# The second product of a fused attention and feed-forward kernel, made product by product, its last ones in two levels of Strassen

## The chip, the cores and the metric

The kernel runs on one core of a Trainium2 chip. The metric is the device time of one execution in microseconds, taken as the median of several runs. All arithmetic is in 32-bit floats.

## The reference, cut to what matters

For 8 batches and 12 heads, sequence 448, head size 64: q and k are normalised by their root mean square and scaled by gains, softmax attention is taken over them, and its output, 3584 tokens by 768, goes through two products with a squared ReLU between them.

```python
q_n, k_n = rmsnorm(q, g_q), rmsnorm(k, g_k)
attn = softmax(q_n @ k_n.T / sqrt(64))
x = (attn @ v) as [3584, 768]
h = x @ w_in                 # 768 -> 2048
g = maximum(h, 0) ** 2
out = g @ w_out              # 2048 -> 768
```

## The kernel before, in words

**Spans.** The work goes in four spans of two batches. Both products are made by Strassen's scheme (Winograd's form): rows of w, depth and tokens are halved, and seven products of half size, named A11, A12, S2, S1, S3, A22 and S4 after the combination of weights that each uses, replace eight. The combinations of weights are prepared in the attention of span 0 and in its first product and lie in DRAM as w1s and w2s; those of x lie in xT and xC, those of g in gT and gC.

**First product** (`first_product`, matmuls at L1068). For each of eight blocks of 128 hidden units, seven products of three matmuls (128x128 weights, 448 tokens). VectorE and ScalarE empty PSUM, ScalarE applies the ReLU (L1040), GpSimd squares (L1044), VectorE makes the combinations of g (`combine`, L1028 to L1032). In spans 1 and 2 the first pairs of the next span's attention are normalised beside it (`ahead`).

**Second product** (`second_product`, matmuls at L1106). For each of three columns m of 128 output features in each half, seven products of eight matmuls, each eight into one PSUM bank; two banks alternate (`bank`). The order is a list, `uses2`: A11 and A12 for each m, then for each m S2, S1, S3, A22, S4. VectorE adds what comes out to p1, y or ct (L1117 to L1127); a finished block is turned by 32x32 transposes and stored by four DMAs (`deliver`, L1139 and L1142). In span 0 `combine` also runs here, beside the first eight of the products.

**What sets the order.** Everything is recorded in the order in which the Python code issues it, and each engine runs its instructions in that order. `second_product` and `attention` are generators: the main loop at the end takes one step of `attention` (61 steps and some at its end) and then as many matmuls of `second_product` as bring it in proportion to `total`. So the attention of the next span is spread over the second product of this one.

**One pair of heads** in `attention(first)`, i its number: scores of two chunks (L785) with their exponentials on ScalarE (L787), the values of pair i-1 (L862), scores of the other two, the copy of `rest` (L992); then, with product matmuls after each yield: `norm_by_squares(i + 2)`, `transposes(i + 1)`, sums of the probabilities and `finish(i - 1)` (L808 to L810, L898, L900), `squares(i + 3)` (ScalarE, L737), `fold(i)`, `combine_x(i - 1)`, and the two DMA steps from GpSimd's queue: factors to DRAM (L1016) and back, spread over partitions (`spread`, L830). `norm_by_squares` reduces on VectorE (L744), swaps neighbouring groups of 32 partitions by four 32x28 copies (L747), adds, scales (L748, L749), and lets GpSimd take the root and multiply (L750, L752). `fold` reduces the sums over partitions (L817), brings three groups of 32 partitions together by three 32x28 copies (L820), adds, inverts and turns them (L822 to L824). Loads of q, k, v, weights (`load_blocks`, L665, five blocks ahead) and the stores are issued by SyncE in order.

**Last product** (`last_product`, span 3, no attention beside it). It is already in two levels: for columns 0 and 1 each of the seven products is made by seven inner ones of four matmuls on 224 tokens (L1206), column 2 as before (L1234). Its inner sums of g are made by VectorE (`add_g`, L1192), those of weights by GpSimd (`add_weights`, L1180).

Of the kernel before, what the change touches and what calls it, by code (L numbers as in the profile page):

```python
# [10 lines left out]
F32 = mybir.dt.float32  # L11
U32 = mybir.dt.uint32
AF = mybir.ActivationFunctionType
ALU = mybir.AluOpType
# [373 lines left out]
def attention_then_ffn_bounded(  # L388
# [35 lines left out]
    nc = tc.nc  # L424
# [4 lines left out]
    P = 128  # L429
# [209 lines left out]
    written = [0]  # L639
    stream = []  # L640

    uses2 = [(m, i) for m in range(HC) for i in (A11, A12)]
    uses2 += [(m, i) for m in range(HC) for i in (S2, S1, S3, A22, S4)]
    def order_of(span, f):

        return (A11, A12, S2, S1, S3, A22, S4) if span == f == 0 else range(7)

    N1 = HF * 7
    N2 = HC * 7 * (HF // 4)

    def load_blocks(upto):

        while len(stream) < min(upto, NSPAN * (N1 + N2) - N2):
            n = len(stream) % (N1 + N2)
            if written[0] < min(2 * (n // 7 + 1) if n < N1 else 2 * NFC, 2 * NFC):
                return
            sw = loads.tile([P, 4, P], F32, tag="sw", name="sw", bufs=5)
            if n < N1:
                sw = sw[:, 0:HC]
                src = w1s[n // 7, order_of(len(stream) // (N1 + N2), n // 7)[n % 7]].rearrange("p (c m) -> p c m", c=HC)  # L660
            else:
                n -= N1
                m, i = uses2[n // (HF // 4)]
                src = w2s[i, n % (HF // 4), :, :, m * P:(m + 1) * P]
            nc.sync.dma_start(sw, src)  # L665
            stream.append(sw)

# [37 lines left out]
    def norm(i):  # L705
        if i >= NAT:
            squares(i)
            return norm_by_squares(i)
        raw, sq = (places_of(qk, i, n)[:SP] for n in range(2))
        rstd = rstds[i] = small.tile([SP, 2, 2 * NJ], F32, tag="rstd", name="rstd", bufs=4)  # L710
        normed[i] = sq[:, 0], raw[:, 1]
        if i <= 2:
            return normalise_in_turn(nc, raw, sq, rstd, mhalf)
        nc.scalar.activation(sq, raw, AF.Square)
        nc.vector.tensor_reduce(rstd, sq.rearrange("p s (n d) -> p s n d", d=D), AX, ALU.add)  # L715
        nc.vector.tensor_scalar(rstd, rstd, 1.0 / D, 1e-6, ALU.mult, ALU.add)
# [22 lines left out]
    def norm_by_squares(i):  # L739
        raw, qkn = (by_squares(i, n) for n in range(2))  # L740
        NG = S // 32
        half = small.tile([P, 2 * NG], F32, tag="half", name="half")
        other = small.tile([P, 2 * NG], F32, tag="other", name="other")
        nc.vector.tensor_reduce(half, qkn.rearrange("p s g e -> p (s g) e"), AX, ALU.add)  # L744
        for n in range(4):
            m = n ^ 1
            nc.vector.tensor_copy(other[n * 32:(n + 1) * 32], half[m * 32:(m + 1) * 32])  # L747
        nc.vector.tensor_tensor(half, half, other, ALU.add)  # L748
        nc.vector.tensor_scalar(half, half, 1.0 / D, 1e-6, ALU.mult, ALU.add)  # L749
        nc.gpsimd.tensor_tensor(half, half, mhalf, ALU.pow)  # L750
        for s in range(2):
            nc.gpsimd.tensor_tensor(  # L752
                qkn[:, s], raw[:, s],
                half[:, s * NG:(s + 1) * NG].rearrange("p g -> p g ()").to_broadcast([P, NG, 32]), ALU.mult)
        normed[i] = qkn
# [56 lines left out]
    def fold(i):  # L812


        NG = S // 32
        acc, quarters = sums["acc"].rearrange("p h q -> p (h q)"), sums["quarters"]
        nc.vector.tensor_reduce(quarters[:, 0], acc.rearrange("p (n k) -> p n k", k=32), AX, ALU.add,  # L817
                                apply_transpose=True)
        for n in range(1, 4):
            nc.vector.tensor_copy(quarters[0:32, n], quarters[n * 32:(n + 1) * 32, 0])  # L820
        square, turned = sums["square"][:, 0], sums["square"][:, 1]
        nc.vector.tensor_reduce(square[:, 0:2 * NG], quarters[0:32].rearrange("p a n -> p n a"), AX, ALU.add)  # L822
        nc.vector.reciprocal(square[:, 0:2 * NG], square[:, 0:2 * NG])
        nc.vector.transpose(turned, square)  # L824
# [147 lines left out]
    def attention(first):  # L972


        last = first + 2 * NPAIR
        for i in range(first, last + 1):
            if i < last:
                scores(i, 0)
                scores(i, 1)
            if i + 3 < min(last + 2, B * NPAIR):  # L980
                load(i + 3)
            if i == first:
                yield
            if i > first:
                values(i - 1)
            if i < last:
                add_up(i, 1)
                scores(i, 3)
                scores(i, 2)
            if i > first:  # L990
                rest = halves[(i - 1) % 2].rearrange("p h q -> p (h q)")
                nc.scalar.copy(rest, rests[i - 1])  # L992
                rests[i - 1] = rest
            if i + 2 < last:
                norm_by_squares(i + 2)
            yield
            if i + 1 < last:
                transposes(i + 1)
            if i < min(last, B * NPAIR - 1):
                load_v(i + 1)  # L1000
            yield
            if i < last:
                add_up(i, 2)
                add_up(i, 3)
            if i > first:
                finish(i - 1)
            if i + 3 < last:
                squares(i + 3)
            yield
            if i < last:  # L1010
                fold(i)
            if i > first:
                combine_x(i - 1)
            yield
            if i < last:
                nc.gpsimd.dma_start(sums["out"][i % 2], sums["square"][0:2 * S // 32, 1])  # L1016
                spread(i)
            yield
# [15 lines left out]
    def first_product(work, span):  # L1034
# [9 lines left out]
                nc.gpsimd.tensor_tensor(g, g, g, ALU.mult)  # L1044

        for f in range(HF):
            n = span * (N1 + N2) + f * 7
            order = order_of(span, f)
            g11, g12 = gT[:, f, 0:S], gT[:, f, S:2 * S]
            g21, g22 = gT[:, HF + f, 0:S], gT[:, HF + f, S:2 * S]  # L1050
# [39 lines left out]

    def second_product(work, span):

        B11, B21, B22 = gT[:, 0:HF, 0:S], gT[:, HF:, 0:S], gT[:, HF:, S:2 * S]
        T1, T2, T4, T3 = gC[:, 0], gC[:, 1], gC[:, 2], gT[:, 0:HF, S:2 * S]
        rhs_of = {A11: B11, S2: T2, S1: T1, S3: T3, A12: B21, A22: T4, S4: B22}
        n = span * (N1 + N2) + N1
        add = nc.vector.tensor_tensor
        done = []
        turn[0] += 1

        p1s = {}
        for j, (m, i) in enumerate(uses2):
            ps = bank("ps")
            for c in range(HF):
                load_blocks(n + 5)
                nc.tensor.matmul(ps, stream[n][:, c % 4], rhs_of[i][:, c], start=c == 0, stop=c == HF - 1)  # L1106
                n += c % 4 == 3
                if c == HF // 2 - 1 and done:
                    yield
                    deliver(work, span, *done.pop())  # L1110
                if span == 0 and j < 8 and c % 4 == 1:
                    combine(j % 4 * HF // 4 + c // 4, (j // 4,))
                if c < HF - 1:
                    yield
            if i == A11:
                p1s[m] = work.tile([P, S], F32, tag="p1", name="p1", bufs=HC)
                nc.scalar.copy(p1s[m], ps)  # L1117
            elif i == S2:
                add(p1s[m], p1s[m], ps, ALU.add)
            elif i == S1:  # L1120
                y = work.tile([P, S], F32, tag="y", name="y", bufs=1)
                add(y, p1s[m], ps, ALU.add)
            else:
                ct = work.tile([P, S], F32, tag="ct", name="ct", bufs=1)
                add(ct, p1s[m] if i in (A12, A22) else y, ps, ALU.add)
                if i == S3:
                    add(p1s[m], p1s[m], ps, ALU.add)  # L1127
                done.append((ct, m + (HC if i in (S3, A22) else 0), 1 if i in (S3, S4) else 0))
            yield
        if done:  # L1130
            deliver(work, span, *done.pop())
            yield


    rows = out.rearrange("(b g t) n -> b t g n", b=B, t=32)

    def deliver(work, span, ct, col, t, queues=(nc.sync,), part=slice(0, S // 32), kept=2):
        osb = work.tile([P, S // 32, 32], F32, tag="osb", name="osb", bufs=kept)[:, part]
        nc.vector.transpose(osb.rearrange("p g n -> p (g n)"), ct[:, part.start * 32:part.stop * 32])  # L1139
        for i in range(0, P, 32):  # L1140
            queue = queues[i // 32 % len(queues)]
# [224 lines left out]
    for span in range(NSPAN - 1):  # L1366
# [5 lines left out]
        with tc.tile_pool(name="second_product", bufs=2, reuse_waits="tile") as work:  # L1372
# [2 lines left out]
            places.append(qkT[:, 1])  # L1375
            halves[:] = [work.tile([P, 2, S // 2], F32, tag=f"half{m}", name="half", bufs=1) for m in range(2)]
            sums_for(work)
            total, done, most = HC * (7 * HF + 4) - 20, 0, 10 * NPAIR + 1
            for u, _ in enumerate(attention(nxt)):
                while done < total * min(u + 1, most) // most + 3 * max(u + 1 - most, 0):  # L1380
                    next(rest)
# [108 lines left out]
```

## Time and profile before

| what | value |
| --- | --- |
| time, median of 3 runs | 1353.98 us (1352.47 to 1356.12) |
| profiled execution | 1352.32 us, span 1350.1 us |
| PE busy | 1329.7 us of the span |
| second product and attention, spans 0, 1, 2 | 196.8, 196.9, 197.0 us |
| matmul 128x128x448, as two records | 0.376 us each in the chain |
| small copies of 32x28, L747 and L820 | 144 of 174 ns and 108 of 339 ns |
| exponential 128x896, L787 | 915 ns |
| root on GpSimd, L750 | 4869 ns |

A matmul of 32-bit floats shows as two records on PE. The profile's matmul durations overlap each other (543 ns on average where the next one starts 376 ns later), so the times between starts are what counts. PE is TensorE, PEld its weight loads, DVE is VectorE, ACT ScalarE, POOL GpSimd, SP SyncE. An instruction's idle time before it names what released it.

### The profile page before, as it was taken

The numbers are of one execution on the slowest core, as the hardware profiler recorded it, in microseconds if no ns is written. First come the engines' busy times: TensorE is split into PE (matmuls) and PEld (weight loads), VectorE is DVE, ScalarE is ACT, GpSimd is POOL, SyncE is SP. The second block draws the span as 40 slices with busy tenths as digits, with TensorE's granted clock in tenths as the row PEclk, the third lists the DMA queues.
The fourth block names the chain that finished last, engine by engine and source line by source line (L and its number), as shares of the span: only waits on it lengthen the run. The fifth ranks groups of instructions, "written<-read, shape, count | busy, mean of one in ns | idle before, by whom it ended". The sixth has DMA issues, their size and how long they took to land.

```text
span 1350.1 us, 17275 instructions
## 1 busy us (share of the span) xinstructions
PE 1329.7 (98%) x5786; PEld 671.6 (50%) x5786; DVE 873.4 (65%) x1537; ACT 431.8 (32%) x681; POOL 619.4 (46%) x504
## 2 busy tenths in 40 slices
PE   8999999999999999999999999999999999999997
PEld 3333445444444455444444455544444445556887
DVE  6999788599987333568777623457878743336553
ACT  7886466433332011233333111223333201111000
POOL 5767533466564122646556212446656412422452
PEclk9999999999999999999999999999999999999999
DMA  9877999655686333345676432345665444431333
GB/s 241 225 217 200 314 360 333 181 131 107 135 151 129 101 87 88 101 114 114 143 146 123 114 97 87 90 112 125 130 123 126 105 102 135 134 88 53 114 101 58
DMA packets 413814, 190.15 MB, mean 141 GB/s; under 512 B 282388, under 2 KB 408724, under 8 KB 413716
## 3 DMA queue, kind: packets, MB, share of 16 engines
q1 hardware_dynamic: 406164, 180.21, 52.0%
q0 software_dynamic: 4736, 8.40, 2.4%
q8 instruction: 48, 0.79, 0.3%
q10 hardware_dynamic: 2816, 0.34, 0.2%
q14 instruction: 50, 0.41, 0.1%
HBM read 155.72 MB, written 33.16 MB: 140 GB/s over the span
## 4 chain that ended last, share of the span: by engine, by line
PE 89%; DVE 5%; ACT 2%; DMA 1%; issue 1%; POOL 0%; SPq 0%; POOLq 0%; DVEq 0%
PE ps L1106 29%; PE pd L1068 10%; PE pa L1068 10%; PE pc L1068 10%; PE sc L785 7%; PE pav L862 7%; PE pb L1068 5%; PE ps L1234 3%; PE pd L1206 2%; PE pc L1206 2%; PE pa L1206 2%; DVE gT L810 1%; PE pb L1206 1%; DVE rstd L715 1%; ACT gT L797 1%
## 5 line engine op out<-in xcount | busy, mean ns | idle before, releaser
L1106 PE MATMUL ps<-gT,sw 128*128 128x448 f32 x576 | 225.8, 543 | 0.0
L1044 POOL TENSOR_TENSOR gT<-gT 128x448 f32<-128x448 f32 x96 | 94.1, 982 | 284.8 <-ACT gT L1040 284.8
L750 POOL TENSOR_TENSOR half<-half,mhalf 128x28 f32<-128x28 f32 x36 | 175.3, 4869 | 74.6 <-DVE half L749 74.0
L1106 PE MATMUL ps<-gC,sw 128*128 128x448 f32 x432 | 170.1, 543 | 0.0
L1106 PEld LDWEIGHTS ps<-gT,sw 128*128 128x128 f32 x576 | 107.5, 190 | 113.9 <-issue 110.1
L1068 PE MATMUL pa<-xT,sw 128*128 128x448 f32 x384 | 155.0, 540 | 0.6 <-ACT p L1072 0.6
L1040 ACT ACTIVATE gT<-gT 128x448 f32<-128x448 f32 x96 | 55.3, 576 | 313.4 <-DVE gT L1083 313.4
L1106 PEld LDWEIGHTS ps<-gC,sw 128*128 128x128 f32 x432 | 80.6, 190 | 86.3 <-issue 83.2
L787 ACT ACTIVATE pr<-sc 128x896 f32<-128x896 f32 x87 | 77.5, 915 | 124.1 <-PE sc L785 124.1
L785 PE MATMUL sc<-qkT 64*64 64x448 f32 (+1 forms) x1152 | 109.8, 496 | 0.0
L1068 PEld LDWEIGHTS pa<-xT,sw 128*128 128x128 f32 x384 | 72.8, 190 | 72.7 <-issue 70.1
L583 POOL TENSOR_TENSOR gC<-gC 128x384 f32<-128x384 f32 x64 | 76.2, 1208 | 62.2 <-DVE gC L579 60.4
L1083 DVE TENSOR_TENSOR gT<-z,pd 128x448 f32<-128x448 f32 x32 | 19.8, 619 | 97.8 <-PE pd L1068 97.7
L1068 PE MATMUL pd<-xT,sw 128*128 128x448 f32 x192 | 77.9, 542 | 1.3 <-DVE z L1075 1.3
L1068 PE MATMUL pd<-xC,sw 128*128 128x448 f32 x192 | 77.5, 540 | 1.3 <-DVE gT L1083 1.3
L830 POOL DMA_DIRECT2D xT<-factors x72 | 38.0, 532 | 88.4 <-DMA factors<-square 56.8
L1068 PE MATMUL pb<-xC,sw 128*128 128x448 f32 x192 | 77.5, 540 | 0.1
L1068 PE MATMUL pc<-xC,sw 128*128 128x448 f32 x192 | 77.4, 539 | 0.0
L1068 PE MATMUL pc<-xT,sw 128*128 128x448 f32 x192 | 77.4, 539 | 0.0
L752 POOL TENSOR_TENSOR qk<-qk,half 128x448 f32<-128x448 f32 x72 | 75.9, 1074 | 2.8
L862 PE MATMUL rest<-pr,vt 64*64 64x448 f32 x348 | 72.7, 537 | 0.0
L862 PE MATMUL pav<-pr,vt 64*64 64x448 f32 x348 | 72.7, 537 | 0.0
(233 smaller groups left out, 2159.2 us busy)
## 6 DMA issues: line engine op xcount, KB each, us to landing
sw<-w1s SPq DMA_DIRECT2D x224, 192.0 KB, 2.4
sw<-w2s SPq DMA_DIRECT2D x126, 256.0 KB, 3.3
w1s<-gC SPq DMA_DIRECT2D x8, 1344.0 KB, 7.1
w2s<-gC SPq DMA_DIRECT2D x8, 1344.0 KB, 6.3
out_dram<-osb SPq DMA_DIRECT2D x184, 56.0 KB, 1.8
qk<-in_q_dram SPq DMA_DIRECT2D x144, 56.0 KB, 3.4
qk<-in_k_dram SPq DMA_DIRECT2D x144, 56.0 KB, 2.8
xT<-factors POOLq DMA_DIRECT2D x72, 112.0 KB, 3.4
```

The lines of the kernel that those rows point to most:

```text
L583: nc.gpsimd.tensor_tensor(*[blocks_of(n)[:, place_of(n, i)] for i in (dst, x, y)], op)
L750: nc.gpsimd.tensor_tensor(half, half, mhalf, ALU.pow)
L752: nc.gpsimd.tensor_tensor(qkn[:, s], raw[:, s], half[:, s * NG:(s + 1) * NG].rearrange("p g -> p g ()").to_broadcast([P, NG, 32]), ALU.mult)
L785: nc.tensor.matmul(sc[part, h, 0:n], qkT[rows, 0, 1, keys], qkT[rows, 0, 0, of], start=True, stop=True)
L787: nc.scalar.activation(pr, sc[:, :, 0:n], AF.Exp)
L862: nc.tensor.matmul(into, vs[i][rows, h, c, :], probs[i, c][rows, h, :], start=(c == 0), stop=(c == NF), skip_group_check=True)
L1040: nc.scalar.activation(g, src, AF.Relu)
L1044: nc.gpsimd.tensor_tensor(g, g, g, ALU.mult)
L1068: nc.tensor.matmul(ps, stream[n + at][:, c], rhs[:, c], start=first and c == 0, stop=c == HC - 1, skip_group_check=not first)
L1106: nc.tensor.matmul(ps, stream[n][:, c % 4], rhs_of[i][:, c], start=c == 0, stop=c == HF - 1)
L1206: nc.tensor.matmul(ps, lhs[:, c], rhs[:, c], start=first and c == 0, stop=c == HK - 1, skip_group_check=not first)
L1234: nc.tensor.matmul(ps, weights_of(o, m, c // HK)[:, c % HK], rhs_of[i][:, c, part], start=c == 0, stop=c == HF - 1)
```

## The change

The second product goes product by product: for each of A11, A12, S2, S1, S3, A22, S4 the three columns m. The first `FIRST[span]` products (6, 5, 5) are made as before; the remaining ones, one in span 0 and two in spans 1 and 2, in two levels for columns 0 and 1 and plainly for column 2. Their weights for columns 0 and 1 are loaded whole into parts of gC that are free by then (`load_set`), inner combinations go to free rows of gT. The steps of the attention are shared over the first products alone (`total`). The four copies of `norm_by_squares` and the three of `fold` go from VectorE to ScalarE. What followed them is cut off into `scale_by_squares`, which comes after `transposes(i + 1)`, and `factors_of`, which comes after `combine_x` and just ahead of the factors' DMA.

```diff
+    FIRST = (6,5,5)
+    order2 = (A11, A12, S2, S1, S3, A22, S4)
...
+            plan += [(w2s[i, k, :, :, m * P:(m + 1) * P], 2 * NFC) for o, i in enumerate(order2)
+                     for m in range(HC) if o < FIRST[span] or m == HC - 1 for k in range(HF // 4)]
...
     def norm(i):
         if i >= NAT:
             squares(i)
-            return norm_by_squares(i)
+            norm_by_squares(i)
+            return scale_by_squares(i)
...
         for n in range(4):
             m = n ^ 1
-            nc.vector.tensor_copy(other[n * 32:(n + 1) * 32], half[m * 32:(m + 1) * 32])
+            nc.scalar.copy(other[n * 32:(n + 1) * 32], half[m * 32:(m + 1) * 32])
+        spare["halves", i] = half, other
+
+    def scale_by_squares(i):
...
         for n in range(1, 4):
-            nc.vector.tensor_copy(quarters[0:32, n], quarters[n * 32:(n + 1) * 32, 0])
+            nc.scalar.copy(quarters[0:32, n], quarters[n * 32:(n + 1) * 32, 0])
+
+    def factors_of(i):
...
             if i + 1 < last:
                 transposes(i + 1)
+            if i + 2 < last:
+                scale_by_squares(i + 2)
...
             if i < last:
+                factors_of(i)
                 nc.gpsimd.dma_start(sums["out"][i % 2], sums["square"][0:2 * S // 32, 1])
...
+        def load_set(o):
+            if o < end:
+                for k, (m, h) in enumerate(((0, 0), (0, 1), (1, 0), (1, 1))):
+                    nc.sync.dma_start(tiles[o][k], w2s[order2[o], h, :, :, m * P:(m + 1) * P])
+
+        def add_g(o, k):
...
+                dst, x, y = ((t1, b12, b11), (t2, b22, t1), (t3, b22, b12), (t4, b21, t2))[k]
+                nc.vector.tensor_tensor(dst, x, y, sub)
+
+        def add_weights(o):
...
+                nc.gpsimd.tensor_tensor(s1, a21, a22, add)
+                nc.gpsimd.tensor_tensor(a21, a11, a21, sub)
...
+        for o, i in enumerate(order2):
...
+            if o < first:
+                for m in range(HC):
+                    ps = bank("ps")
+                    for c in range(HF):
+                        load_blocks(n + 5)
+                        nc.tensor.matmul(ps, stream[n][:, c % 4], rhs_of[i][:, c], start=c == 0, stop=c == HF - 1)
+                        n += c % 4 == 3
+                        at = (o * HC + m) * HF + c
+                        if span == 0 and at < 8 * HF and at % 4 == 1:
+                            combine(at // 4 % HF, (at // 4 // HF,))
...
+                        if o == first - 1 and c == 5:
+                            if m < 2:
+                                load_set(first + m)
+                            for k in ((0, 1), (2,), (3,))[m]:
+                                add_g(first, k)
+                            if m == 2:
+                                add_weights(first)
...
+            pa = ps_s.tile([P, 2, 512], F32, tag="s", name="pa")[:, 0, left]
+            yield from run(pa, a11, lambda c: b11[:, c])
+            nc.scalar.copy(z, pa)
+            nc.gpsimd.tensor_tensor(a11, s1, a11, sub)
+            nc.gpsimd.tensor_tensor(s4, a12, a11, sub)
+            for k in range(3):
+                add_g(o + 1, k)
+            send(o)
...
+            third = work.tile([P, S], F32, tag="ct", name="ct", bufs=1)
+            nc.vector.tensor_tensor(third, base[2], ps, add)
+            pb = ps_o.tile([P, S], F32, tag="o", name="pb")[:, left]
+            yield from run(pb, a11, lambda c: t2[c])
+            nc.vector.tensor_tensor(z, z, pb, add)
...
+            pc = bank("pc")[:, left]
+            yield from run(pc, s1, lambda c: t1[c])
...
+            add_weights(o + 1)
...
+            pd = ps_o.tile([P, S], F32, tag="t", name="pd")[:, left]
+            yield from run(pd, a21, lambda c: t3[c])
...
+            yield from run(pa, a12, lambda c: b21[:, c], False)
...
+            yield from run(pd, a22, lambda c: t4[c], False)
...
+            yield from run(pc, s4, lambda c: b22[:, c], False)
...
-            total, done, most = HC * (7 * HF + 4) - 20, 0, 10 * NPAIR + 1
+            total, done, most = FIRST[span] * HC * HF - (20 if FIRST[span] == 7 else 6), 0, 10 * NPAIR + 1
```

## The prediction

> **What bounds the kernel now.** I read first the page's busy times, then its chain of work, then one stage after another.
>
> ```profile
> PE 1329.7 (98%) x5786; PEld 671.6 (50%) x5786; DVE 873.4 (65%) x1537; ACT 431.8 (32%) x681; POOL 619.4 (46%) x504
> PE 89%; DVE 5%; ACT 2%; DMA 1%; issue 1%; POOL 0%; SPq 0%; POOLq 0%; DVEq 0%
> ```
>
> TensorE is busy 98% of the span and the chain that ends last runs 89% on it, so a product that needs fewer columns is time saved, if TensorE is still fed. The busy times by stretch give the second-product stages of spans 0 and 1, then 15 us of span 0:
>
> ```profile
> 261.00:457.80 196.80, 196.80 (x1112) 91.83 (x1111) 164.46 (x317) 62.82 (x88) 104.13 (x79) 1.00 0.62 126
> 582.00:778.90 196.90, 196.90 (x1112) 91.96 (x1111) 148.01 (x290) 60.98 (x85) 101.18 (x78) 1.00 0.59 126
> 306.00:321.00 15.00, 15.00 (x91) 7.00 (x90) 14.51 (x29) 4.72 (x7) 8.70 (x6) 1.00 0.51 80
> ```
>
> After the stretch and its length come PE, PEld, DVE, ACT and POOL. PE has no gap in either stage, although VectorE is nearly full in the first pairs of span 0. What the new form costs is already in the trace: the last product of the kernel is made in it. The timeline of PE:
>
> ```profile
> 1226.13 1.68 PE L1206 MATMUL pa<-gT,qk 128*128 128x224 f32 x8
> 1227.64 6.18 PE L1234 MATMUL ps<-gT,qk 128*128 128x448 f32 x16
> 1233.66 1.68 PE L1206 MATMUL pb<-xC,qk 128*128 128x224 f32 x8
> ...
> 1242.74 1.68 PE L1206 MATMUL pa<-gT,wb 128*128 128x224 f32 x8
> ```
>
> From pa to the next pa is 16.61 us. Eight records of 224 columns take 1.51 us, sixteen of 448 take 6.02 (a matmul is two records: 0.376 us each at 448, 0.189 at 224). Half the columns cost half, and the weight loads of 0.190 us don't slow it.
>
> Then one pair of the attention inside the second product of span 1:
>
> ```profile
> 643.64 1.73 PE L785 MATMUL sc<-qkT 64*64 64x448 f32 x16
> 644.68 0.92 ACT L787 ACTIVATE qkT<-sc 128x896 f32<-128x896 f32 x1 [1.19 <-PE sc L785]
> 647.82 1.31 PE L785 MATMUL sc<-qkT 64*64 64x224 f32 x16
> 650.07 0.53 ACT L992 COPY half<-rest 128x448 f32<-128x448 f32 x1
> 656.54 1.10 DVE L817 TRANSPOSE_TENSOR_REDUCE quarters<-acc 128x28 f32<-128x896 f32 x1
> 657.67 0.57 DVE L820 COPY quarters<-quarters 32x28 f32<-32x28 f32 x3
> 659.03 1.73 PE L785 MATMUL sc<-qkT 64*64 64x448 f32 x16
> ```
>
> A pair starts with its scores at 643.64, the next at 659.03. The fold of the sums (L817) ends 1.4 us before that: VectorE runs a whole pair behind.
>
> [...] the 112x16 activation of L725 took 216 ns. [...] three copies of L820 took 0.57 us alone and 1.48 at 640.87 beside GpSimd's multiply L752 (mean 339 ns each). [...] Here the small factors DMA lands in 2.7, the spread in 3.4.
>
> **The change, part by part.**
>
> 1. Five products in two levels: S4 in span 0, A22 and S4 in spans 1 and 2. A plain product is 24 matmuls: 24 x 0.7515 = 18.04 us. A two-level one takes 16.61 to 16.73 in the last product (periods between its 448-wide blocks); I take 16.67. Saved 1.37 each, **6.8 us** in all, on the bound engine.
>
> 2. Their extra sums. Per product VectorE gets four 128x896 subtractions (L1192, 1.1 to 1.5 us) and some 4 us of smaller ones, about 10 us in 16.7; GpSimd four 128x512 sums (1.27 each) and three of 0.66. In the last product the same load cost TensorE 0.1 us here and there, which is in 16.67. Taken as 0, bounds 0 to 0.5 each: the cover is the 6.0 us block of the third column, made before pb needs the new weights. The new weight DMAs (4 x 256 KB) are issued one product ahead, and stream loads fall by the same number of blocks.
>
> 3. Order. Product by product instead of column by column changes neither matmuls nor evictions: 0. Deliveries bunch in the second product (A12) and S3, so SyncE holds 2.1 us of out DMAs per delivery ahead of the next q and k loads, and these feed the squares on ScalarE. In before such loads came up to 6.6 us into a pair and the squares 14.3 us into it, without harm to PE. Taken as 0, bounds 0 to 2.
>
> 4. The attention is packed tighter, since it ends before the two-level products. In before the first scores of two pairs are 14.64 or 15.40 us apart, with 12 or 13 product matmuls between them, so the pair itself takes 14.64 - 12 x 0.7515 = 5.62. Now 114 matmuls are shared over 61 steps, 5 to a pair: 9.34 x 0.7515 + 5.62 = **12.64 us** in spans 1 and 2; 138 in span 0 give 11.31 and 14.1 us. That is no gain or loss on TensorE; the question is whether the others follow. VectorE had 148.0 us in span 1. Less 12 x 1.7 of small copies, less 12.7 of evictions and deliveries that move behind the attention, plus 5 for the first subtractions of g: about 120 in 160 (120 matmuls, 90 us, and 12.5 pairs, 70), 75% as before. GpSimd: 4.83 + 2.1 + 0.6 + 1.05 and some 2.7 of waiting for the factors, 11.3 of 12.64.
>
> 5. Small copies. ScalarE gets 7 per pair, 1.5 us; it has 5.1 of 15 us busy. But they wait for VectorE in ScalarE's queue. Behind the three of the fold stand the exponentials of the next pair, for which TensorE waits. The chain from a pair's first score at 0: ScalarE ends the copy of rest at 6.96 (650.60), its four copies at 7.8; VectorE's root sums, 0.37, end at 8.2; two adds 1.08 + 1.27, finish 1.25, fold 1.10 and gaps, 4.9: 13.1; three copies and two handoffs of 0.05: **13.85**. The next exponential would start at 12.64 + 1.04 = 13.68, so it is 0.2 late, and 0.8 to 1.4 late where an eviction (0.6) and a delivery (0.64) lie in the chain. TensorE notices when a score buffer isn't free: the third scores start 4.18 into the pair (647.82), so the exponential may start at 3.2 instead of 1.04, 2.1 late. The margin is 0.7 to 1.9 us. Other chain: square ends 14.8, GpSimd is free of its multiply at about 15.3, factors and spread take 3.1 + 3.7, landed at 22.1, 9.5 into the next pair; wanted at 11.3. I take 0.7 us of stalls in spans 1 and 2 together, bounds 0 to 12. In span 0 VectorE also combines g over the first 64 matmuls; before, its fold slipped to 3.0 us into the next pair with no stall. The same slip now delays the exponential to about 5.0, where 3.2 is allowed; but the pair's work falls by 1.7 us of copies to about 14.3 in 14.1, so I let it slip by half: 0.6 us, bounds 0 to 5.
>
> 6. The first product. Four times (two in spans 1 and 2 each) a norm sits before z. In before:
>
> ```profile
> 541.57 0.78 DVE L747 COPY other<-half 32x28 f32<-32x28 f32 x4
> 542.69 0.61 DVE L1075 TENSOR_TENSOR z<-p,pb 128x448 f32<-128x448 f32 x1
> 543.36 2.52 PE L1068 MATMUL pd<-xT,sw 128*128 128x448 f32 x6
> ```
>
> pd came 0.18 late (a block takes 2.44 instead of 2.25 in the chain), because z empties its bank. The copies become 4 x 0.21 plus two handoffs of 0.05, 0.94 in place of 0.78: 0.2 us more each time, **0.8 us** lost. Bounds 0 and, at 0.3 per copy, 2.
>
> Sum: -6.8 + 0.7 + 0.6 + 0.8 = **-4.7 us**. The profiled run took 1352.32 us, span 1350.1 plus 2.2; its span becomes 1345.4. The median of the runs shown is 1.66 above that run: 1353.98 - 4.7 = **1349.3 us**.
>
> **Rivals.**
>
> A. Nearly all of the gain arrives: no stall at all, 1347.2. For it: PE idles nowhere in the stages of before, even behind a full VectorE. I count it with the forecast.
>
> B. Half or more is eaten by waits in the tight pairs: late factor DMAs (landings of the spread up to 5.6 us, against margins of 1.8, and 0.7 where GpSimd has a difference of x to make) and the slip in span 0. 3 to 6 us go: 1350 to 1353, about 1352. Against it: these delays fall in few pairs.
>
> C. Slower: the exponentials queued behind the fold's copies become a ring with VectorE. It decides once the chain of 13.85 grows by more than the 0.7 to 1.9 us of margin, in every pair: from there each us is a us per pair. Copies of 0.35 instead of 0.21 add 1.0[...]. Then 0.5 us in 32 pairs, 16 us, less 6.8 - 0.8: 1354 + 10 = 1364. Against it: the chain is caught again in each pair, as the root sums wait for TensorE's scores, not for the fold.
>
> D. The two-level products don't reach 16.7, since they follow an attention whose last finish shares VectorE with the new subtractions: 1 us in each of three stages, 1352. For it: finish, three differences of x and the subtractions add up to 8 us in the first of them; against it, pa, third column and the last values take 10.2.
>
> **How the numbers follow.** Forecast with A 0.60 (1346.5 to 1350.5), B and D 0.24, C 0.16. A measurement of this kernel tells about 0.3%, 4 us, from no change. Faster by more than that, under 1349.9: most of the forecast, a little of B, 0.57. Slower, over 1358: most of C, 0.14. The rest 0.29. Range 1346.3 to 1357.
>
> **What would show it.** Right: PE blocks of 16.7 us at the ends of spans 0 to 2, pairs 12.6 and 14.1 us apart, no wait of PE for an activation, four pd blocks 0.4 us late. Wrong: pairs longer than that in spans 1 and 2 with the first exponential more than 3.2 us after the first score (C), waits of VectorE for the spread (B), gaps before pb or pd of the two-level products (D), copies on ScalarE well over 0.21 us.

## The result, and the profile after

| | median | lowest to highest | ratio to before (95% interval) |
| --- | --- | --- | --- |
| before, 20 runs | 1353.93 us | 1351.97 to 1356.12 | |
| after, 20 runs | 1351.57 us | 1349.20 to 1354.89 | 0.9982 (0.9976 to 0.9989) |
| after, the profiled execution | 1349.56 us, span 1347.7 | | |

The changed kernel is 2.4 us faster by the medians, and the profiled spans differ by as much (1350.1 to 1347.7; the profiled times differ by 2.8, so 0.4 us lie outside the spans). Forecast were 4.7. The sign is right, the time lies in the range; half of the gain is missing. How much is missing differs from one set of executions to the next: run 1 below, the same kernel on another chip, is 3.2 us ahead by its ratio and 4.1 by the medians, and its profiled span is 1345.8.

The page's lines of busy time and the head of its chain of work, of the kernel after:

```profile
PE 1325.4 (98%) x5906; PEld 694.1 (52%) x5906; DVE 843.6 (63%) x1325; ACT 485.3 (36%) x938; POOL 666.4 (49%) x539
PE 83%; DVE 7%; ACT 3%; DMA 2%; issue 2%; POOL 1%; SPq 0%; DVEq 0%; POOLq 0%; ACTq 0%
```

TensorE still has 98%, but the chain that ends last now runs 83% on it instead of 89: more of the way to the end leads over waits for the others. VectorE has 30 us less than before, net of its new subtractions, ScalarE 54 more. The second-product stages of spans 0, 1 and 2, cut from the first matmul after the first product to the first matmul of the next one (stretch, length, then the busy time of PE, PEld, DVE, ACT and POOL, each with its number of instructions, the granted clock, DMA share, GB/s), after:

```profile
263.23:456.92 193.69, 193.44 (x1130) 95.17 (x1130) 149.56 (x246) 77.25 (x162) 110.84 (x85) 1.00 0.58 126
583.97:775.81 191.84, 191.78 (x1154) 99.64 (x1154) 138.71 (x226) 76.60 (x162) 119.41 (x92) 1.00 0.59 127
904.00:1096.18 192.18, 191.99 (x1153) 99.53 (x1153) 139.50 (x226) 76.59 (x162) 119.42 (x92) 1.00 0.55 121
```

With the same cuts before has 194.4 in each of the three. The stages win 0.7, 2.6 and 2.2 us, 5.5 in all, which is what steps 1 and 5 of the prediction come to, and TensorE has almost no gap in them. So what is missing in this execution was lost elsewhere. The same cut over the whole span (us; the last column holds the last product and the end; every number is a difference of starts in the timeline of PE):

| | to the first product | first | second, span 0 | first | second, 1 | first | second, 2 | first | last, end |
| --- | --- | --- | --- | --- | --- | --- | --- | --- | --- |
| before | 132.28 | 130.91 | 194.41 | 126.73 | 194.40 | 126.72 | 194.40 | 126.28 | 123.95 |
| after | 132.85 | 130.38 | 193.69 | 127.04 | 191.85 | 128.19 | 192.18 | 126.28 | 125.23 |
| difference | +0.57 | -0.53 | -0.72 | +0.31 | -2.55 | +1.47 | -2.22 | 0.00 | +1.28 |

The new products, in span 1's timeline of PE and VectorE (start, duration; in brackets the idle time before and what ended it):

```profile
750.12 1.68 PE L1160 MATMUL pb<-gT,gC 128*128 128x224 f32 x8
754.86 0.39 DVE L1237 TENSOR_TENSOR gT<-p,pd 128x224 f32<-128x224 f32 x1 [0.36 <-PE pd L1160]
756.17 1.68 PE L1160 MATMUL pd<-gT,gC 128*128 128x224 f32 x8
766.73 1.68 PE L1160 MATMUL pb<-gT,gC 128*128 128x224 f32 x8
```

From pb to pb it is 16.61 us, as from pa to pa in the last product of before. VectorE's subtraction L1237 frees the bank for TensorE's second pd block. VectorE was ready for it 0.36 us before its input came, and it ended at 755.25, 0.92 before that block began. So VectorE could come about 1.2 us later here before TensorE would wait (0.05 us taken off for the handoff, an estimate; in run 3 below, where TensorE does wait, L1237 ends at 1083.05 and pd starts at 1083.11): that is its lead.

One pair of the attention in the same stage:

```profile
633.40 1.10 DVE L824 TRANSPOSE_TENSOR_REDUCE quarters<-acc 128x28 f32<-128x896 f32 x1
633.81 1.73 PE L792 MATMUL sc<-qkT 64*64 64x448 f32 x16
634.59 0.69 ACT L827 COPY quarters<-quarters 32x28 f32<-32x28 f32 x3 [4.30 <-DVE quarters L824]
635.19 0.90 ACT L794 ACTIVATE qkT<-sc 128x896 f32<-128x896 f32 x1
638.00 1.31 PE L792 MATMUL sc<-qkT 64*64 64x224 f32 x16
646.20 1.73 PE L792 MATMUL sc<-qkT 64*64 64x448 f32 x16
```

The next pair begins 12.39 us later. From 595.60 to 722.04, ten pairs, the mean is 12.64; in span 0, from 276.35 to 418.26, it is 14.19. The fold ends 0.7 us after the first scores instead of 1.4 before the next ones, the three copies follow, and behind them the exponential starts 1.38 after the score began instead of 1.04. TensorE takes the third scores 4.19 into the pair without a wait. That is the chain of the prediction's step 5, inside its margin. The other pairs of spans 1 and 2 have their first exponential 1.05 to 3.40 after the score; where it came 3.06 and 3.40 after, TensorE waited 0.1 and 0.2.

### The profile page after: what moved, and what is told of

Same layout as the page of the kernel before. It is cut to its first block, busy times and chain, and to the rows that moved or that the text cites. A ratio compares the mean times of both kernels' runs of the same rounds, so it can differ in the third digit from the quotient of the medians.

```text
span 1347.7 us, 17639 instructions
## 1 busy us (share of the span) xinstructions
PE 1325.4 (98%) x5906; PEld 694.1 (52%) x5906; DVE 843.6 (63%) x1325; ACT 485.3 (36%) x938; POOL 666.4 (49%) x539
## 4 chain that ended last, share of the span: by engine, by line
PE 83%; DVE 7%; ACT 3%; DMA 2%; issue 2%; POOL 1%; SPq 0%; DVEq 0%; POOLq 0%; ACTq 0%
PE ps L1175 19%; PE pd L1083 10%; PE pa L1083 10%; PE pc L1083 10%; PE sc L792 6%; PE pav L874 6%; PE pb L1083 5%; PE ps L1352 3%; PE ps L1219 2%; PE pd L1324 2%; PE pa L1324 2%; PE pc L1324 2%; PE pc L1160 1%; PE pd L1160 1%; PE pa L1160 1%
## 5 line engine op out<-in xcount | busy, mean ns | idle before, releaser
L757 POOL TENSOR_TENSOR half<-half,mhalf 128x28 f32<-128x28 f32 x36 | 185.3, 5148 | 83.2 <-DVE half L756 73.7
L1175 PE MATMUL ps<-gT,sw 128*128 128x448 f32 x432 | 169.3, 545 | 0.0
L1175 PE MATMUL ps<-gC,sw 128*128 128x448 f32 x336 | 131.4, 545 | 0.0
L1175 PEld LDWEIGHTS ps<-gT,sw 128*128 128x128 f32 x432 | 80.1, 190 | 87.5 <-issue 86.1
L1175 PEld LDWEIGHTS ps<-gC,sw 128*128 128x128 f32 x336 | 62.4, 190 | 68.1 <-issue 66.3
L827 ACT COPY quarters<-quarters 32x28 f32<-32x28 f32 x108 | 22.9, 212 | 138.0 <-DVE quarters L824 136.3
```

## The experiments

Ratios are against the kernel before on the same chip. Runs 1 to 4, 5 to 8 and 9 to 12 share a chip each, so ratios are safely compared within such a group only. "Stage" is a second-product stage as cut above.

| run | median us | ratio | stages 0, 1, 2 | first products of spans 1, 2 |
| --- | --- | --- | --- | --- |
| 1 the change, again | 1349.56 | 0.9976 (0.9966 to 0.9985) | 193.68, 191.76, 191.59 | 127.22, 126.98 |
| 2 early load | 1349.50 | 0.9968 (0.9956 to 0.9980) | 193.68, 191.71, 191.86 | 126.98, 126.98 |
| 3 copies on VectorE | 1357.62 | 1.0034 (1.0021 to 1.0047) | 195.14, 194.28, 196.01 | 126.72, 127.59 |
| 4 no two-level product | 1356.53 | 1.0022 (1.0015 to 1.0029) | 195.00, 194.40, 194.40 | 126.99, 126.98 |
| 5 norms outside pairs on VectorE | 1348.65 | 0.9956 (0.9942 to 0.9971) | 193.68, 191.54, 192.45 | 126.90, 126.68 |
| 6 = 5 and 2 | 1347.34 | 0.9947 (0.9933 to 0.9962) | 193.70, 192.06, 191.72 | 126.69, 126.68 |
| 7 every small copy twice | 1362.94 | 1.0070 (1.0051 to 1.0088) | 195.31, 194.54, 195.86 | 128.86, 128.88 |
| 8 before, with the copies alone | 1353.96 | 1.0002 (0.9994 to 1.0011) | 194.40, 194.40, 194.40 | 126.98, 126.98 |
| 9 = 6, `FIRST` 5,5,5 | 1351.73 | 0.9992 (0.9983 to 1.0001) | 196.56, 191.79, 191.72 | 126.69, 126.67 |
| 10 = 6, `FIRST` 7,5,5 | 1351.18 | 0.9986 (0.9979 to 0.9993) | 195.00, 193.62, 192.96 | 126.69, 126.69 |
| 11 = 6, fold's copies on VectorE | 1353.30 | 1.0010 (1.0002 to 1.0019) | 192.97, 196.23, 193.23 | 126.72, 126.72 |
| 12 before again, once | 1352.82 | | 194.40, 194.41, 194.40 | 126.72, 126.72 |

The median of before was 1353.61 beside runs 1 to 4, 1354.00 beside 5 to 8, 1352.78 beside 9 to 12.

**Runs 1 and 4: what do the two-level products bring?** Run 1 is the changed kernel as it is.

> The changed kernel once more, for what repeats in its profile. Theory: TensorE gains 1.37 us in each of five products less small stalls, so the second-product stages of spans 0, 1, 2 are again about 193.7, 191.9 and 192.2 us long where they were 194.4; the 1.1 us wait of pa for sw in the first product of span 2 and the late end after the last matmul (1.3 us more than before) are chance and come and go. Time 1351.5, 1348 to 1353 by the run. Rival: both waits are part of the change and stand again at the same place with the same length.

Run 4 keeps the new order and the copies on ScalarE, and makes all seven products plainly (its `total` is 148 matmuls, where before shared the attention over 160, so its pairs are somewhat tighter than those of before):

```diff
-    FIRST = (6,5,5)
+    FIRST = (7,7,7)
```

> FIRST = (7,7,7): product by product and the small copies on ScalarE, but no product in two levels. Theory: the order and the copies give nothing on TensorE; without the two-level products the second-product stages are 194.4 us again, with the norms 0.3 us late per span: 1354 to 1355, ratio 1.000 to 1.001. Rival: the new order itself brings or costs something (deliveries in bunches, weights behind them): 1352 or less, or 1357 or more.

The stage of span 1, first of run 4, then of run 1:

```profile
585.80:780.20 194.40, 194.40 (x1105) 90.87 (x1105) 125.74 (x211) 76.52 (x160) 102.51 (x78) 1.00 0.58 127
```

```profile
584.12:775.88 191.76, 191.76 (x1153) 99.70 (x1153) 138.67 (x226) 76.53 (x162) 119.10 (x92) 1.00 0.59 127
```

PE's busy time equals the stretch in both: no gap. Two products save 2.64 there and 2.81 in span 2, and with span 0's (195.00 - 193.68 = 1.32) the five bring 6.8 us, step 1's number, in place. The extra 13 us of VectorE and 17 of GpSimd per stage cost TensorE nothing. By the medians the form is worth 7.0 us (1356.53 to 1349.56). Run 4 itself is 2.9 slower than before. Its profiled span is 2.4 longer: 0.6 in span 0's stage, 0.5 in the first products of spans 1 and 2, 0.6 up to the end of the first product (133.44 + 130.37 against 132.28 + 130.91) and 0.7 at the end (124.66), of which more below.

**Runs 2, 5 and 6: where is it lost?** The table of stages names the start, span 2's first product and the end. The start, in the end of the first attention, which the prediction never looked at. Before, ScalarE and PE:

```profile
124.37 2.21 ACT L797 ACTIVATE gT<-sc,rstd 112x448 f32<-112x448 f32 x4
124.61 2.48 PE L876 MATMUL tot<-gT,ones 112*64 112x448 f32 x12
...
132.28 2.15 PE L1068 MATMUL pa<-xT,sw 128*128 128x448 f32 x5
```

and after:

```profile
123.87 2.48 PE L888 MATMUL tot<-gT,ones 112*64 112x448 f32 x12
...
125.68 0.92 ACT L748 COPY other<-half 32x28 f32<-32x28 f32 x4 [2.74 <-DVE half L745]
...
127.45 2.19 ACT L804 ACTIVATE gT<-sc,rstd 112x448 f32<-112x448 f32 x4
128.12 2.16 PE L863 MATMUL pav<-gT,vt 112*64 112x448 f32 x7 [0.27 <-ACT gT L804]
```

The norm of the next span's first pair (L958 of the changed kernel calls it) stands ahead of the last exponentials of this attention. Its four copies take 0.92 us, but ScalarE first stands still 2.74 us for VectorE's sums, and behind the copies wait a conversion (L589, 0.93 us at 126.62) and the exponentials (L804). These start 3.6 us after the same tot block, where before they started 0.2 ahead of it. From tot to the first product it is 8.98 us instead of 7.67: +1.31 (the start is only 0.57 later, since the tot block itself came 0.74 earlier in this execution), of which 0.53 come back in the first product, where pd then waits 0.71 instead of 1.27 for a subtraction of VectorE. Run 5 gives only the norms outside the spans' pairs back to VectorE:

```diff
     def norm(i):
         if i >= NAT:
             squares(i)
-            norm_by_squares(i)
+            norm_by_squares(i, nc.vector.tensor_copy)
...
-    def norm_by_squares(i):
+    def norm_by_squares(i, copy=nc.scalar.copy):
...
-            nc.scalar.copy(other[n * 32:(n + 1) * 32], half[m * 32:(m + 1) * 32])
+            copy(other[n * 32:(n + 1) * 32], half[m * 32:(m + 1) * 32])
```

> The four copies of a norm stay on VectorE where the norm is made outside the attention of a span (at the end of the first attention and beside the first products); inside it, and for all folds, they stay on ScalarE. Theory: at the end of the first attention ScalarE's copies wait for VectorE's reduction and the last exponentials stand behind them, which puts the first product off by 1.3 us, of which 0.6 come back at its first pd; and four pd blocks come 0.1 us less late. So the first product of span 0 starts 7.7 us after the last-but-one tot block as before (9.0 in the changed kernel), and the time falls by 1 to 1.3 us against the changed kernel, to about 1349 to 1350. Rival: TensorE makes this time good elsewhere and the time stays within 0.3 us.

From tot (126.55) to the first product (134.22) it takes 7.67 again, and the first products of spans 1 and 2 come to 126.90 and 126.68 (126.69 and 126.68 in run 6) instead of 126.98: both losses come from these copies. (The profiled starts of runs 5 and 6 themselves, 134.22 and 133.69, are later than the changed kernel's 132.85; what made them late was not shown, but their mean granted clocks are 0.996 and 0.997 against its 0.999, see the last section.) The longer first product of span 2 is another matter. SyncE's queue and PE at its start, in the kernel after:

```profile
777.05 3.98 SPq L1260 DMA_DIRECT2D out_dram<-gT  x8
781.12 7.68 SPq L665 DMA_DIRECT2D sw<-w1s  x6
785.96 2.49 PE L1083 MATMUL pa<-xT,sw 128*128 128x448 f32 x6 [0.97 <-DMA sw<-w1s]
```

The last of the seven products delivers two columns at once, eight output DMAs of 0.5 us; in before there were four (1.88 us of SyncE from 780.26 on). Until they are issued no weights are asked for, and TensorE waits 1.0 us for the fifth block. In run 1 the same block comes in time; in run 3 it waits 0.6. Run 2 asks for the weights ahead of these outputs:

```diff
             late += [(into[m], m + where[0], where[1]) for m in (1, 0)]
+        load_blocks(n + 5)
         send(end)
```

> The next weight block is asked for ahead of the eight output DMAs at the end of each second product. Theory: the fifth weight block of the first product stands behind these DMAs in SyncE's queue and is late at some span ends in some executions; asked for earlier it is never late, so pa waits for no weights, the first products of spans 1 to 3 take 126.3 to 127.1 us, and the time falls by 0.5 to 1.1 us against the changed kernel beside it, to about 1350.7. Rival: the wait was one chance landing, or the output DMAs then delay something else, and the time is the same within 0.3 us.

There is no such wait at this place in the profiles of runs 2 and 6, but run 1 had none either, and run 2 is not distinct from run 1 (0.9968 against 0.9976, intervals overlap). A wait that comes in some executions only is too small for these rounds. Run 6 has the edits of runs 5 and 2:

> As the run before, and the next weight block asked for ahead of the last output DMAs of each span. Theory: both add up, 1348.5 to 1349.5, the shortest of all. Rival: the early load gives nothing beyond the chance of one landing, and the two kernels are alike within 0.5 us.

It has the best ratio of the study, 0.9947 (6.7 us by the medians), not distinct from run 5 beside it (0.9956). It is the version to keep, though it was not timed on the chip of runs 9 to 12.

**Runs 3 and 11: were the copies on ScalarE needed?**

```diff
-            nc.scalar.copy(other[n * 32:(n + 1) * 32], half[m * 32:(m + 1) * 32])
+            nc.vector.tensor_copy(other[n * 32:(n + 1) * 32], half[m * 32:(m + 1) * 32])
...
-            nc.scalar.copy(quarters[0:32, n], quarters[n * 32:(n + 1) * 32, 0])
+            nc.vector.tensor_copy(quarters[0:32, n], quarters[n * 32:(n + 1) * 32, 0])
```

> The seven small copies of a pair go back to VectorE, in the new places; the rest is as in the changed kernel. Theory: in spans 1 and 2 VectorE has room either way, so no change there; the four norms beside the first product lose 0.1 us less each; in span 0 VectorE gets 1.0 to 1.7 us more per pair while it combines g and slips further behind, but no exponential stands behind it any more, so TensorE loses 0 to 1 us. Time within 1 us of the changed kernel, rather faster (1350.5 to 1352). Rival, that the copies on ScalarE are needed: VectorE becomes the bound of the tight pairs, the pairs of spans 1 and 2 grow beyond 12.7 us and the time is 1355 or more.

Slower than before, 8 us behind run 1. The pairs of span 1 show no wait; the price is paid after them. The end of stage 2 in run 3:

```profile
1073.74 0.71 DVE L912 TENSOR_TENSOR xT<-half,xT 128x448 f32<-128x448 f32 x1 [4.08 <-DMA xT<-factors]
...
1082.70 0.35 DVE L1237 TENSOR_TENSOR gT<-p,pd 128x224 f32<-128x224 f32 x1
...
1083.11 1.99 PE L1160 MATMUL pd<-gT,gC 128*128 128x224 f32 x8 [2.05 <-DVE gT L1237]
```

VectorE runs behind through the attention, folds late, then stands 4.08 us for the spread of those late factors, and carries the delay into the subtractions of the first two-level product. TensorE's second use of the bank waits for L1237, the very instruction that was some 1.2 us ahead in the changed kernel. By the starts of its blocks TensorE is late by 2.63 us in span 1 and 2.22 in span 2, and in span 0 it waits 1.6 for a finish (L910). The copies themselves: a mean of 468 ns in the fold on VectorE here (339 in before), 212 on ScalarE. What makes VectorE's copies longer here than in before was not shown. Run 11 starts from run 6 and gives VectorE only the fold's three copies:

```diff
-            nc.scalar.copy(quarters[0:32, n], quarters[n * 32:(n + 1) * 32, 0])
+            nc.vector.tensor_copy(quarters[0:32, n], quarters[n * 32:(n + 1) * 32, 0])
```

> The best kernel with the fold's three copies back on VectorE; the norm's four stay on ScalarE within the attention. Theory: what the copies on VectorE cost in e3 is the last fold beside GpSimd's work (its three copies took 2.29 us there) and the backlog that VectorE carries into the first two-level product; so most of the 6 to 8 us come back with the fold alone: 1351 to 1355. Rival: the ring through ScalarE is the dearer, and without the fold's copies in front of the exponentials the time falls by some tenths: 1346.5 to 1347.3.

Again pd waits for L1237, 4.0 us in two places, and the ratio is 1.0010. So most of the harm, and of the part's use, lies in the fold's 108 copies. The thought that their place ahead of the exponentials might cost more than they free falls for spans 1 and 2. In span 0 the profile speaks for it: there the stage takes 192.97 in run 11, against 193.68 to 193.70 with the copies on ScalarE, and has no wait. A kernel with the fold's copies on VectorE in span 0 alone was not run.

**Run 8: the copies without the products.** The kernel before with both copies on ScalarE and the two functions cut as in the change:

```diff
-            nc.vector.tensor_copy(quarters[0:32, n], quarters[n * 32:(n + 1) * 32, 0])
+            nc.scalar.copy(quarters[0:32, n], quarters[n * 32:(n + 1) * 32, 0])
+
+    def factors_of(i):
```

> The kernel before with only the small copies on ScalarE and the split functions; order and products as before. Theory: the copies cost TensorE 1.3 us at the end of the first attention, 0.6 of it given back, and 0.1 at each of four norms; pairs of 14.6 us have room for the rest: 1354.7 to 1355.5, so that they account for at least half of what the order of products without two levels lost (2.9). Rival: the order of products is what lost it, and this kernel is within 0.5 us of the one before.

Ratio 1.0002, and the interval reaches from -0.8 to +1.5 us, so the time can't confirm a cost of 0.7 to 1.5. The stages can: 8.99 us from tot to the first product (7.67 in before) and 126.98 in each first product (126.72), while every second-product stage takes 194.40, as before. Alone the copies bring nothing; what they free is VectorE's time, and it is the two-level products that need it (run 3).

**Run 7: how near is the ring?** Every small copy is made twice on ScalarE, the second time to the same place:

```diff
-            nc.scalar.copy(quarters[0:32, n], quarters[n * 32:(n + 1) * 32, 0])
+            for _ in range(2):
+                nc.scalar.copy(quarters[0:32, n], quarters[n * 32:(n + 1) * 32, 0])
```

> Each of the seven small copies is made twice, 1.5 us more per pair on ScalarE. The theory of the ring (the next exponentials behind the fold's copies, TensorE behind these): the exponentials of spans 1 and 2, which start 1.1 to 2.7 us after the scores where 3.2 is allowed, start 0.7 to 1.5 later, so that a few pairs stall by some tenths, the worst by 1 us; with 0.7 at the end of the first attention and 4 times 0.9 at the norms in all 5 to 9 us more than the changed kernel: 1357 to 1361. Rival, that ScalarE's room hides it in the attention: only the norms and the first attention show it, 1354 to 1356.

1362.94, a little above what was expected. From the waits of PE in run 7 (total us, times, longest):

```profile
PE pd L1085 <- DVE z L1092: 5.3, 5, 1.3
PE sc L793 <- ACT pr L795: 4.0, 11, 1.4
```

The changed kernel has 1.3 us in one place and 0.4 in two. 0.65 us more in the fold's chain turns TensorE's wait for exponentials from 0.4 into 4.0 us, and the four norms beside the first products, with 0.97 us more of copies, come 1.1 to 1.2 late each. In the timeline the waits appear where an exponential starts 3.3 us or more after the first score; those at 2.1 to 3.0 cost nothing that counts. That is rival C's mechanism at its point of decision, and the changed kernel is short of it.

**Runs 9 and 10: is span 0 rightly split?** From run 6, the first with 5, the second with 7 plain products in span 0:

```diff
-    FIRST = (6,5,5)
+    FIRST = (5,5,5)
```

```diff
-    FIRST = (6,5,5)
+    FIRST = (7,5,5)
```

> The best kernel so far (norms outside the attention on VectorE, early weight load) with FIRST = (5,5,5): A22 in two levels in span 0 too. Theory: TensorE saves another 1.37 us, but the pairs of span 0 shrink from 14.1 to 12.6 us of matmuls while VectorE still combines g in them: 9.3 of attention, 4.1 of differences and about 1 of evictions make 14.4 a pair over the first five; the exponentials wait behind a fold that slips 1.5 us or more each pair beyond the 2 us of room, and TensorE stalls some 4 to 8 us: 1350 to 1355, 2 to 6 us above e6. Rival: VectorE catches up afterwards as it did in the kernel before, and the time falls to about 1346.

> The same with FIRST = (7,5,5): no two-level product in span 0. Theory: span 0 loses 1.37 us of saving and gets most of its 0.6 us of stall back or not (the stage was 195.0 with the plain order and 193.7 with one two-level product): 1.0 to 1.4 us above e6. Rival: the two-level product of span 0 pays nothing since VectorE bounds that stage, and the times are alike.

With one product more in two levels span 0's pairs become tighter, and the stage takes 196.56 instead of 193.70. At its worst place the scores of a pair begin at 339.04, the exponential starts 5.6 us later at 344.64, and TensorE waits 2.2 us for it, until 345.59. Without any two-level product in span 0 the stage takes 195.00. By the stages six is right for span 0. The times of runs 9 and 10 can't show it: run 6 was not timed beside them, and the stages of spans 1 and 2 in run 10, which have its code, were 1.6 and 1.2 longer in the profiled execution.

**Run 12: the end.** From the last matmul's end the span goes on for 7.2 us in before and 8.5 in after, with the same code for the last product.

> The kernel before once more, for what repeats in its profile. Theory: the stages repeat to 0.1 us (second products 194.4, first products 126.7), while the end, 7.2 us from the last matmul to the end of the span where the others so far show 7.5 to 9.2, is a lucky landing and comes out at 7.5 to 9. Rival: 7.2 again, so that the longer end belongs to the change.

The thought that before had been lucky falls: the second profile of before ends like the first (123.77 in the last column against 123.95). Runs 6, 9 and 10 end as before does (123.9 to 124.0), runs 1, 2 and 7 late (125.0 to 126.0), the others lie between. In after the output's bytes are gone by 1344 and the span ends at 1347.7; in before they are gone by 1347 and it ends at 1350.1. So over half a microsecond lies behind the output. What decides it stays open.

## Why the prediction was right or wrong

1. **Five products, -6.8: right**, to 0.1, in size and place (runs 1 and 4). This step rested on periods between blocks that the trace of before already held.
2. **Extra sums, 0: right.** Rival D's place is real, but VectorE holds it with a lead of about 1.2 us; runs 3 and 11 show what happens when it is lost. "The new weight DMAs ... fall by the same number of blocks" was right for loads and missed the deliveries at the end of the stage.
3. **Order, 0: too low.** I looked at the loads of q and k behind output DMAs, and not at the next first product's weights behind the last eight of them: 1.0 us in the profiled execution, 0 in run 1. Run 4 (order, copies and slightly tighter pairs) has 1.0022 where run 8 (copies alone) has 1.0002, which are two chips; their profiles differ by 0.6 in span 0's stage, which is one late exponential as in step 5, and by 0.3 at the end, and no more was found.
4. **Pairs of 12.64 and 14.1: right**, 12.64 and 14.19. Single pairs lie between 12.39 and 13.43.
5. **Copies, 0.7 and 0.6 of waits: right in place and kind;** that the sizes agree is partly chance. Spans 1 and 2 lose 0.2 and 0.5 in after and 0.1 in all in run 1 (the excess over 191.6). Span 0 has 195.0 in runs 4 and 10, all plain, where 194.4 is full speed, 0.6, and in after at its tightest place (scores at 332.68, exponentials at 336.16) TensorE waits 0.16 and 0.19; with the fold's copies on VectorE (run 11) the stage is 0.7 shorter. The prediction saw the exponential of span 0 slip to about 5.0 and let it slip by half; measured were 3.5, in one pair. In spans 1 and 2 it had them at most 1.4 late, and the latest was 2.4. The bound of 3.2 us for the exponential came out at 3.3 in run 7. The 0.21 us per copy, here and in step 6, was an estimate, with the 216 ns of L725 for its only measured ground; in after the copies take 212 ns on ScalarE, L748 and L827 alike.
6. **Norms beside first products, 0.8:** the mechanism is right, the size 0.26 per span, 0.5 in all. **The step that failed is its count**, "four times": I went through the places where a norm sits before z, and did not ask where else `norm` is called. A fifth, at the end of the first attention, was the dearest: 1.31 us, 0.8 net of what the next wait gives back (a sixth, in the last block of span 0's first product, delayed nothing). The price is not that of four copies but of ScalarE's in-order wait of 2.74 us with exponentials behind it.
7. **The end, no term at all:** +1.28 in the profiled execution, +1.1 in run 1, open.

The sum for the profiled execution, by the table of stages: -5.5 in the three second products (-6.8 for the form, less the waits of step 5), +0.04 for start and first product of span 0 (+1.31 - 0.53 - 0.74), +1.8 in the first products of spans 1 and 2 (norms 0.5, weights some 1.1), +1.3 at the end: -2.4. The forecast's -4.7 lacked the weights and the end, 2.4 us together, and had in norms and waits about what was found. For run 1's profile, against the same before, the sum is -4.3, near the forecast: -6.2 in the three second products, no wait for weights, +0.8 in the first products of spans 1 and 2, +1.1 at the end. So the weights' part of the loss belongs to some executions only.

The result is rival B's number, "half or more is eaten by waits", but not in the tight pairs and not by late factors: outside them, where the change only passed through. The prediction gave 0.57 to a time under 1349.9 and 0.29 to one that can't be told from no change; the latter came.

## What to carry to other kernels

When an instruction is moved to another engine's queue, list every call of the function that issues it, and at each price what stands behind it while it waits for its input; here the wait was 2.74 us and the work 0.92. A form whose period can be read in the trace of before may be taken at that period (16.61 us in before and in after), if the engine that feeds it keeps its lead: look for the smallest stretch between the end of the feeder's instruction and the start of what needs it, and add the feeder's idle time before that instruction. Look at what a stage's last output DMAs put off on the same queue: here eight of them held SyncE for 3.98 us ahead of the next weights, and TensorE waited 1.0 us in one profile and not at all in another. Asking for the weights first gave no distinct gain (0.9968 against 0.9976).

## What was not expected of the hardware

After some of its waits TensorE ran on at half speed. Stretches of three microseconds within 3 us after such a wait, run 11 in span 1, then run 3 in spans 1 and 2 (PE, PEld, DVE, ACT, POOL, then the granted clock):

```profile
760.00:763.00 3.00, 3.00 (x9) 2.70 (x8) 1.31 (x2) 0.00 (x0) 2.61 (x2) 0.50 0.31 52
```

```profile
761.00:764.00 3.00, 2.81 (x15) 2.81 (x16) 2.55 (x4) 0.00 (x0) 2.92 (x3) 1.00 0.70 165
1086.00:1089.00 3.00, 3.00 (x12) 2.81 (x11) 0.81 (x2) 0.00 (x0) 1.00 (x2) 0.67 0.00 0
```

In run 11 nine records are seen in 3 us, at a clock of 0.50, where run 3 has fifteen at 1.00. In run 3's span 2 the eight records of 224 columns of pc take 2.99 us at that clock (1084.89 to 1087.88), 0.37 each, instead of 1.51 and 0.19. After a wait of 2.63 us in run 3 the clock stayed at 1.00, after one of 2.22 it fell. In the clock's own record each such stretch is 3.41 us long (759.62 to 763.03 in run 11, 1084.55 to 1087.96 in run 3), so by an estimate from this length and the clock of 0.50 it costs some 1.7 us.

The length of the wait alone does not decide it. In the first attention TensorE waits before the same instruction (PE pt, L768 in before, L775 in the other two, from 19.4 us on in the changed kernel) for 2.29 us in before, 1.94 in the changed kernel and 1.92 in run 2. In before and in the changed kernel the clock stays at 1.00, in run 2 a half-speed stretch follows. The changed kernel, then run 2, in stretches as long as the half-speed one:

```profile
16.62:20.03 3.41, 2.74 (x16) 0.88 (x12) 1.62 (x5) 3.41 (x6) 1.64 (x1) 1.00 1.17 273
20.03:23.45 3.42, 2.15 (x12) 1.02 (x12) 3.35 (x5) 2.69 (x5) 1.88 (x1) 1.00 1.09 347
```

```profile
18.45:21.86 3.41, 1.49 (x12) 0.55 (x8) 3.24 (x6) 3.41 (x7) 1.81 (x2) 1.00 1.13 303
21.86:25.27 3.41, 3.41 (x11) 1.22 (x12) 3.18 (x7) 1.70 (x5) 0.10 (x1) 0.50 1.09 348
```

The first number after the length is TensorE's busy time. What decides whether the clock falls was not shown, and no run was made to test it.

In run 3 the half speed made a wait of 2 us cost nearly double: the stage of span 2, with 2.22 us of wait and a half-speed stretch, is 4.4 us longer than in run 1 (196.01 against 191.59), that of span 1, with 2.63 us and none, 2.5 (194.28 against 191.76). A stretch in the first attention, as in run 2, puts off what follows by some 1.7 us, by the same estimate. So the time up to the first product can't be compared between a profile that has one there and a profile that has none; in before and after the clock is 1.00 from 6.4 us to TensorE's last matmul.

This may also be part of the spread between executions. One such stretch lowers the mean clock of an execution by 0.0013 (1.7 of some 1350 us, an estimate), and within one kernel a mean clock lower by 0.001 goes with some 1.0 to 1.2 us more (20 executions of the changed kernel, 45 of before). The mean over the changed kernel's 20 executions is 0.9969, over those of before on the three later chips 0.9976 to 0.9980. So some of the gain that the medians miss may lie here and not in any wait of the tables above; that was not shown.
